# Forty-two sums of weight quarters on GpSimd instead of VectorE, under a new table of places for all instructions

## The chip, the cores and the metric

The kernel runs on one core of one Trainium2 chip. The metric is device time in microseconds (us) for one execution. TensorE (PE) multiplies, VectorE (DVE) and ScalarE (ACT) work element by element and move results out of PSUM, GpSimd (POOL) makes masks and issues some of the transfers, and SyncE (SP) issues the others. Each engine executes its instructions in the order in which the program lists them; what an instruction needs from another engine it waits for, and everything behind it on its engine waits with it.

## The reference

Threshold attention on 8 batches of 8 heads (576 positions, 64 columns a head), and behind it a feed-forward layer with a quick GELU on the 4608 rows that come out, all in float32:

```
scores = scale * np.matmul(q, k.transpose(0, 1, 3, 2))          # 8 x 8 x 576 x 576
thresh = np.max(scores, axis=-1, keepdims=True) - tau
scores = np.where(scores >= thresh, scores, -1000000000.0)
scores = scores - np.max(scores, axis=-1, keepdims=True)
attn = np.exp(scores)
attn = attn / (np.sum(attn, axis=-1, keepdims=True) + 1e-09)
x = np.matmul(attn, v)   -> rearranged to 4608 x 512
h = x @ w_in                                                    # 512 -> 2048
g = h * (1.0 / (1.0 + np.exp(-1.702 * h)))
return g @ w_out                                                # 2048 -> 512
```

## The kernel before, in words

**Attention.** The 64 heads are worked through as 32 pairs `n`, two heads at a time. For a pair, `scores` (L839) multiplies keys by queries into PSUM tiles `ps`; ACT copies them to SBUF (`keep`, L856), as five tiles `sT[n, t]`: four of 128x1152 and one of 128x576. DVE takes maxima of the tiles (`in_groups`, L879, into `part`), which become one row of thresholds for the pair; a transfer spreads that row over all partitions. Then each tile has the row added or subtracted: by DVE (`sub`, L961), or, for two of the five tiles in 25 of the pairs, by an accumulating DMA that GpSimd issues (`add_mb`, L954). Then ACT pushes everything below the threshold far down (`mask`, L968) and takes exponentials (`exps`, L972). PE multiplies them with the values into `pv`, and with ones into `den` (`by_values`, L983). DVE divides and writes the result into a tile `xT`, 128 x 4 x 256, one for each block of 256 rows; there are six such tiles. In the 25 pairs whose sums are not made by PE, DVE adds up the exponentials instead (L869).

**Feed-forward.** The 4608 rows are 18 blocks of 256. The layer `w_in` gives `hps`, ACT or DVE applies the GELU, and `w_out` gives `ops`. Blocks are multiplied with seven products in place of eight on half-size quarters (`P1` to `P7`), which needs sums and differences of quarters of the weights and of `x`. Lines L1163, L1174, L1238, L1411 and L1566 are products of the first layer, L1675 and L1719 of the second. While the pairs run (to about 950 us) blocks lie between the scores and values of the pairs and keep PE busy while the softmax of the next pair is on its way; from 950 us the last six blocks run alone (the tail, `TAIL` = 12). A PE that changes between 64x64 matmuls (scores, values) and 128x128 matmuls (feed-forward) does so in stretches: the order is scores and values mixed, then a stretch of feed-forward, then the next pair.

**The sums of weight quarters.** The tail uses a deeper form of the seven products, for which further sums of weight quarters are wanted: 7 for the first layer (`left1`) and 7 for the second (`right2`), each made by three additions or subtractions of 128x512. That is 14 x 3 = 42 operations, all in the function `scrap_sum` (L1464 to L1481). They are made between 280 and 810 us, and SP stores the results to DRAM (`extra_out`, `scrap_out`), from where the tail loads them (`extra_in`). Four of the fourteen are made beside blocks 2 and 3, in a free `xT` tile (`EARLY_EXTRAS`); ten beside blocks 4, 6, 8 and 10, in one tile `scrap` (`LATE_EXTRAS`), where each sum waits until the store of the one before has read the tile:

```
    nc.vector.tensor_tensor(out=o, in0=a, in1=b, op=op)          # L1481, the sum itself
    ...
    a = task("DVE", 0.6, FIRST, scrap_sum, second_layer, x, k, after=freed + [t_ready[-1], a])
    a = task("SP", 0.55, FIRST, scrap_out, second_layer, x, k, after=[a], take=RING[0])
```

**Weights at the start.** `w_in` and `w_out` come in through two staging tiles (`load_w`, L757, whose tiles the program calls `w_out` and `arena`), and are split into parts by `cv_...` steps on ACT and DVE, among them `cv_whole` (L785) and a step at L792 on DVE, L767 and L771 on ACT. All of this lies in the first 120 us.

**What sets the order.** All work is a list of tasks: engine, planned cost, rank, function, what it comes after, and which buffer it takes and gives back. `run_in_order` (L499) first writes a number from a table, `PLACES`, with 4767 entries, over the rank of each task, and then runs a planner: it simulates the engines with the planned costs, and each engine that is free takes the ready task with the lowest number. The instructions are issued in the order that comes out; the engines then run it as written, so the planned costs matter only through the order.

Of the kernel before, what the change touches and what calls it, by code (L numbers as in the profile page):

```python
# [21 lines left out]
P = 128  # L22
# [10 lines left out]
def kernel(  # L33
# [96 lines left out]
    for x in ("raw0", "raw1", "qkT0", "qkT1", "mb"):  # L130
# [113 lines left out]
        "keep1": 0.0,  # L244
        "keep4": 0.0,
# [7 lines left out]
        "silu4": 0.0,  # L253
        "x_sum": 0.0,
# [3 lines left out]
    STEP = {  # L258
        "add_mb": 0.0,
        "exps": 0.0,  # L260
        "in_groups": 0.0,
        "keep": 0.0,
        "mask": 0.0,
        "sub": 0.0,
# [14 lines left out]
    ENTER = {True: 0.2, False: 0.22}  # L279
# [27 lines left out]
    def transfer(by, time, a, kind=0, give=(), lag=1.7):  # L307
# [3 lines left out]

    PLACES = """
# [752 lines left out]
    def spread_sums(n):  # L1065
# [4 lines left out]
        nc.vector.transpose(out=rc, in_=r.unsqueeze(2).to_broadcast([P, QB, 32]))  # L1070
        rcs[n] = rc

    xTs = {}

    def cuts(b):

# [1776 lines left out]
```

## Time and profile before

| | |
|---|---|
| time, median of 3 runs | 1220.14 us (1217.45 to 1220.29) |
| profiled execution: time | 1220.53 us |
| profiled execution: span from the first to the last instruction | 1218.7 us, so 1.8 us lie outside |
| granted TensorE clock, mean | 0.997 of full speed |
| instructions in the span | 26167 |

The page is of one execution. A row of the list of groups reads: line of the code, engine, operation, written tile and read tiles with partitions x elements, number of instructions | busy us, mean ns of one | idle us of the engine just before them and what ended most of it. A row of the timeline reads: start in us, length in us, engine, line, operation, number of instructions in a row, and in square brackets how long the engine stood before it and what released it. A row of the stretches (windows) reads: from:to, length, then busy us (and number of instructions) of PE, PE's weight loads, DVE, ACT and POOL, then the granted clock, the busy share of the transfer engines and GB/s. A matmul in the trace is two records of a float32 matmul in the code. Names like `arena` and `w_out` are those of large tiles that hold many things in turn.

### The profile page before, as it was taken

How to read it: one execution, taken by the hardware profiler on the slowest of the kernel's cores; microseconds unless marked ns; L12 is line 12 of the kernel's file. 1: busy time of each engine (PE TensorE's matmuls, PEld its weight loads, DVE VectorE, ACT ScalarE, POOL GpSimd, SP SyncE). 2: the span in 40 equal slices, each digit the busy share in tenths (PEclk: the TensorE clock that was granted, in tenths of full speed). 3: DMA queues.
4: the chain of work that ended last, by engine and by line, in shares of the span. 5: the costliest groups of instructions: out<-in, count | busy, mean ns of one | idle time of the engine just before them, and what ended most of it. 6: DMA issues, size and time to landing. Idle time of an engine off the chain costs nothing.

```text
span 1218.7 us, 26167 instructions
## 1 busy us (share of the span) xinstructions
PE 1196.9 (98%) x10560; PEld 982.3 (81%) x10560; DVE 1067.9 (88%) x1622; ACT 794.1 (65%) x1183; POOL 130.5 (11%) x176
## 2 busy tenths in 40 slices
PE   9898999999999999999999999999999999999998
PEld 6555777788877778777777777777778999999998
DVE  7979998989989888999899877997896799799797
ACT  7999986888686868667875569667882340340340
POOL 0111232110001110012100110011100000000000
PEclk9999999999999999999999999999999999999999
DMA  9856869777555564567735653557623544545443
GB/s 246 227 114 167 205 144 178 150 149 206 132 131 120 132 150 103 126 146 178 152 71 127 168 123 66 142 119 203 159 60 122 181 124 149 172 131 148 141 138 96
DMA packets 220617, 176.56 MB, mean 145 GB/s; under 512 B 148752, under 2 KB 165776, under 8 KB 220368
## 3 DMA queue, kind: packets, MB, share of 16 engines
q1 hardware_dynamic: 197776, 125.42, 38.1%
q0 software_dynamic: 22032, 49.17, 20.2%
q8 instruction: 83, 1.36, 0.5%
q10 hardware_dynamic: 688, 0.30, 0.1%
q14 instruction: 38, 0.31, 0.1%
HBM read 119.53 MB, written 25.84 MB: 119 GB/s over the span
## 4 chain that ended last, share of the span: by engine, by line
PE 78%; ACT 14%; DVE 3%; DMA 3%; issue 2%; POOL 0%; SPq 0%; DVEq 0%; ACTq 0%; POOLq 0%
PE ops L1719 21%; PE pv L983 9%; PE ps L839 8%; PE hps L1411 8%; PE hps L1566 6%; PE ops L1675 6%; PE ps L1411 6%; PE ps L1566 5%; PE ps L1675 5%; ACT arena L968 4%; ACT arena L972 3%; ACT arena L856 2%; PE hps L1238 2%; PE ps L1238 1%; DVE arena L961 1%
## 5 line engine op out<-in xcount | busy, mean ns | idle before, releaser
L879 DVE TRANSPOSE_TENSOR_REDUCE part<-arena 128x36 f32<-128x1152 f32 (+1 forms) x250 | 297.3, 1212 | 21.4 <-ACT arena L856 15.0
L856 ACT COPY arena<-ps 128x576 f32<-128x576 f32 x288 | 171.5, 643 | 54.6 <-PE ps L839 52.1
L968 ACT ACTIVATE arena<-arena 128x1152 f32<-128x1152 f32 (+1 forms) x160 | 168.4, 1063 | 59.3 <-DVE arena L961 55.4
L972 ACT ACTIVATE arena<-arena,shift 128x1152 f32<-128x1152 f32 (+1 forms) x160 | 183.3, 1160 | 2.6
L839 PE MATMUL ps<-arena 64*64 64x288 f32 x2304 | 172.7, 409 | 7.8 <-ACT arena L856 6.2
L1719 PE MATMUL ops<-w_out,arena 128*128 128x256 f32 x768 | 174.6, 381 | 0.8 <-DVE osb L1741 0.4
L1719 PEld LDWEIGHTS ops<-w_out,arena 128*128 128x128 f32 x768 | 144.4, 190 | 26.9 <-issue 4.8
L983 PE MATMUL pv<-arena 64*64 64x288 f32 x2176 | 160.4, 407 | 0.0
L839 PEld LDWEIGHTS ps<-arena 64*64 64x64 f32 x2304 | 81.9, 133 | 70.9 <-ACT arena L856 29.1
L961 DVE TENSOR_TENSOR arena<-arena 128x1152 f32<-128x1152 f32 (+1 forms) x100 | 130.1, 1337 | 2.9 <-DMA arena<-row 2.2
L983 PEld LDWEIGHTS pv<-arena 64*64 64x64 f32 x2176 | 81.1, 133 | 52.7 <-issue 7.9
L1580 ACT COPY arena<-hps 128x512 f32<-128x512 f32 x66 | 38.5, 583 | 114.3 <-PE hps L1566 114.2
L1719 PE MATMUL ops<-arena 128*128 128x256 f32 x464 | 104.4, 380 | 0.7 <-ACT osb L1734 0.7
L954 POOL DMA_DIRECT2D arena<-arena x50 | 55.1, 1317 | 429.2 <-DVE arena L919 245.1
L1719 PEld LDWEIGHTS ops<-arena 128*128 128x128 f32 x464 | 87.9, 190 | 13.8 <-ACT osb L1734 1.1
L869 DVE TRANSPOSE_TENSOR_REDUCE part<-arena 128x72 f32<-128x2304 f32 x25 | 64.2, 2570 | 10.8 <-ACT arena L972 10.5
L1411 PE MATMUL hps<-xT,w_in 128*128 128x256 f32 x256 | 59.4, 382 | 0.1
L1741 DVE SCALAR_TENSOR_TENSOR osb<-ops,osb 128x256 f32<-128x256 f32 x84 | 33.5, 410 | 25.7 <-PE ops L1719 24.6
L1411 PEld LDWEIGHTS hps<-xT,w_in 128*128 128x128 f32 x256 | 48.1, 190 | 9.4 <-issue 2.6
L1452 ACT COPY arena<-hps 128x512 f32<-128x512 f32 x64 | 36.8, 578 | 26.7 <-PE hps L1411 26.5
L899 ACT ACTIVATE other<-red,gap 32x18 f32<-32x18 f32 x100 | 30.7, 307 | 35.9 <-DVE red L888 34.7
L1174 PE MATMUL hps<-xT,w_in 128*128 128x256 f32 x232 | 51.9, 382 | 1.9 <-DVE arena L1180 1.8
(223 smaller groups left out, 2056.8 us busy)
## 6 DMA issues: line engine op xcount, KB each, us to landing
arena<-in_v_dram SPq DMA_DIRECT2D x128, 144.0 KB
arena<-exu SPq DMA_DIRECT2D x63, 256.0 KB
arena<-ext SPq DMA_DIRECT2D x60, 256.0 KB
arena<-arena POOLq DMA_DIRECT2D x25, 576.0 KB, 6.1
arena<-wrow POOLq DMA_DIRECT2D x48, 256.0 KB, 4.5
arena<-in_q_dram SPq DMA_DIRECT2D x112, 72.0 KB
arena<-in_k_dram SPq DMA_DIRECT2D x112, 72.0 KB
arena<-arena POOLq DMA_DIRECT2D x25, 288.0 KB, 7.5
```

The source lines that it names most:

```text
L839: nc.tensor.matmul(ps[ts(c, KT), h, 0:SH], lhsT=mats[n, 1][ts(h, D), ts(j, KT)], rhs=mats[n, 0][ts(h, D), ts(c, SH)], start=True, stop=True,)
L856: nc.scalar.copy(out=sT[n, t][:, u], in_=pss.pop((n, j))[:, :, 0:SH])
L869: nc.vector.tensor_reduce(out=stats[n, ALU.add][:, t * 2 * QB : min(2 * t + 4, NK) * QB], in_=arena2[:, lo : mid + size].rearrange("p (c d ...
L879: nc.vector.tensor_reduce(out=stats[n, op][:, t * 2 * QB : min(2 * t + 2, NK) * QB], in_=sT[n, t].rearrange("p u h (g d) -> p (u h g) d", ...
L961: engine.tensor_tensor(out=s, in0=s, in1=mbs[n].unsqueeze(1).to_broadcast(list(s.shape)), op=ALU.add if n in BY_DMA or n in NEGATED else A ...
L968: nc.scalar.activation(out=s, in_=s, func=AF.Prelu, alpha=STEEP)
L972: nc.scalar.activation(out=s, in_=s, func=AF.Exp, scale=SCALE, bias=shift)
L983: nc.tensor.matmul(o[c][ts(h, D), 0:SH], lhsT=left(j, h)[ts(c, KT)], rhs=sT[n, t][ts(c, KT), u, h, :], start=(j == 0), stop=(j == NK - 1),)
L1411: nc.tensor.matmul(o[:, ts(j, BLK)], lhsT=left[:, c, ts(j, P)], rhs=right[:, c, :], start=(x in (P1, P2, P5) and j + c == 0), stop=(j + c ...
L1566: nc.tensor.matmul(o[:, ts(j, HT)], lhsT=left[:, ts(j, P)], rhs=right, start=(m in (P1, P2, P5) and j == 0), stop=(j == 3), skip_group_che ...
L1675: nc.tensor.matmul(banks3[pos, r][:, 0:HT], lhsT=left[:, j, :], rhs=right[:, j, :], start=(m in (P1, P2, P5) and j == 0), stop=(j == 3), s ...
L1719: nc.tensor.matmul(banks[blk][k][:, ts(o, HM)], lhsT=left[:, j, :], rhs=right[:, j, :], start=(j == 0), stop=(j == HF - 1),)
```

## The change

Three things change in the code.

1. The 42 operations of `scrap_sum` are issued on GpSimd, and their planned cost goes from 0.6 to 1.45.
2. The six `xT` tiles, until now handed out in turn by a pool, become six fixed tiles with a list of free ones (`x_free`): a user takes the first free one and its last user, by the planner, puts it back. Similarly the PSUM banks of one form of the first layer (`product4`, `keep4`) are remembered for each quarter `q` instead of two by turns.
3. The table `PLACES` is new throughout, so the order of nearly everything in the first half of the program is new; behind that the two orders are nearly alike apart from the sums; three of the planner's costs change with it (the transfer of the first two pieces of `w_out` is planned at 5.2 instead of 1.7, one transfer of a threshold row at 2.7 instead of 1.0, and entering one of the matmul modes at 0.0 instead of 0.2). Offsets for single tasks (`AT`) are emptied; `PLACES` overrides them in both programs.

Among the instructions themselves, only the 42 sums change: every engine but DVE and POOL issues the same instructions in another order. The summing of exponentials of two score tiles in one operation on DVE (`PAIRED`, 25 operations 128x72 from 128x2304) is the same in both programs.

```
 def scrap_sum(second, x, k):
 ...
-                places["extra", second, x] = x_home()
+                places["extra", second, x] = x_home((second, x))
 ...
-        nc.vector.tensor_tensor(out=o, in0=a, in1=b, op=op)
+        nc.gpsimd.tensor_tensor(out=o, in0=a, in1=b, op=op)
...
-                    "DVE", 0.6, FIRST, scrap_sum, second_layer, n, k,
+                    "POOL", 1.45, FIRST, scrap_sum, second_layer, n, k,
...
-                a = task("DVE", 0.6, FIRST, scrap_sum, second_layer, x, k, after=freed + [t_ready[-1], a])
+                a = task("POOL", 1.45, FIRST, scrap_sum, second_layer, x, k, after=freed + [t_ready[-1], a])
...
+    x_free, x_ends = list(range(NXT)), {}
...
+                x_free.extend(x_used.pop(key) for key in x_ends.get(i, ()) if key in x_used)
...
+    x_tiles = [const.tile([P, NDC, BLK], FP32, name=f"xT{x}") for x in range(NXT)]
+    x_used = {}
+
+    def x_tile(key):
+        x_used[key] = x_free.pop(0)
+        return x_tiles[x_used[key]]
...
-            places[y] = psM.tile([P, BANK], FP32, name="hps", tag="mo")
+            places["q", q] = psM.tile([P, BANK], FP32, name="hps", tag="mo")
...
-        a = transfer("DMS", W_TIME, a, 2, give=RING[0], lag=1.7 if i else 3.3)
+        a = transfer("DMS", W_TIME, a, 2, give=RING[0], lag=(5.2 if n_in <= i < n_in + 2 else 1.7) if i else 3.3)
...
-        rq = ("POOL", 1.4, "DMW", 1.0) if n in ROWS_BY_POOL else ("SP", 1.0, "DMS", 1.7)
+        rq = ("POOL", 1.4, "DMW", 2.7 if n == 1 else 1.0) if n in ROWS_BY_POOL else ("SP", 1.0, "DMS", 1.7)
...
-    ENTER = {True: 0.2, False: 0.22}
+    ENTER = {True: 0.0, False: 0.22}
...
     PLACES = """
-        114 170 133 238 4 92 157 188 151 49 8 600 155 191 299 353 83 365 180 203 376 143 354 391 326 212
+        20 104 357 14 328 8 81 136 28 23 123 411 41 138 74 150 19 381 57 140 184 223 174 384 99 152
```

What the new table moves is seen where the engines' instructions stand. Five places follow; each row is an operation with the tile it writes, the tiles it reads, the size and how many stand in a row. The line numbers of the changed program are 15 to 21 lower.

The first is SP's queue near 40 to 80 us, where the last pieces of `w_in`, the first two of `w_out` (L757, L736 in the changed program), and the keys, queries and values of the pairs are loaded. Before:

```order
L757 DMA w_out<-in_moe_w_in_dram 128x2047
L704 DMA arena_90<-in_q_dram 32x18x32 x4
L704 DMA arena_90<-in_k_dram 32x18x32 x4
L715 DMA arena_90<-in_v_dram 64x576 x4
L704 DMA arena_90<-in_k_dram 32x18x32 x4
L757 DMA w_out<-in_moe_w_out_dram 128x2047
L757 DMA arena<-in_moe_w_out_dram 128x2047
```

And after:

```order
L736 DMA w_out<-in_moe_w_in_dram 128x2047 x4
L694 DMA arena_90<-in_v_dram 64x576 x4
L736 DMA w_out<-in_moe_w_out_dram 128x2047
L736 DMA arena<-in_moe_w_out_dram 128x2047
L683 DMA arena_90<-in_k_dram 32x18x32 x2
L683 DMA arena_90<-in_q_dram 32x18x32 x4
L694 DMA arena_90<-in_v_dram 64x576 x4
```

The two loads of `w_out` now stand ahead of the next pair's keys and queries instead of behind them.

The second is DVE between 83 and 93 us, with the threshold subtractions of a pair (L961, L940 after) and the weight steps (L785 and L792, L771 after). Before:

```order
L792 SCALAR_TENSOR_TENSOR w_in<-w_out,w_in 128x512 x2
L792 SCALAR_TENSOR_TENSOR w_in<-arena,w_in 128x512
L961 TENSOR_TENSOR arena<-arena 128x1152
L785 TENSOR_SCALAR w_out<-w_out 128x512
L879 TENSOR_REDUCE part<-arena_90 128x36
L961 TENSOR_TENSOR arena<-arena 128x1152
L879 TENSOR_REDUCE part<-arena_90 128x18
L961 TENSOR_TENSOR arena<-arena 128x1152
```

And after:

```order
L771 SCALAR_TENSOR_TENSOR w_in<-arena,w_in 128x512
L940 TENSOR_TENSOR arena<-arena 128x1152
L771 SCALAR_TENSOR_TENSOR w_in<-arena,w_in 128x512
L940 TENSOR_TENSOR arena<-arena 128x1152 x2
L858 TENSOR_REDUCE part<-arena_90 128x36 x2
L858 TENSOR_REDUCE part<-arena_90 128x18
```

The first `cv_whole` of a `w_out` piece (L785 on tile `w_out`) no longer stands between the pair's subtractions.

The third is PE between 342 and 370 us: the end of a first-layer block (L1238, L1223 after), second-layer products `ops` (L1719, L1704 after), and the values `pv` (L983, L962 after) and scores `ps` (L839, L818 after) of the next two pairs. Before:

```order
L1238 MATMUL ps<-xT,arena_90 128x128 x16
L1719 MATMUL ops<-w_out,arena 128x256 x4
L983 MATMUL pv<-arena_90 64x288 x8
L839 MATMUL ps<-arena_90 64x288 x8
L983 MATMUL pv<-arena_90 64x288 x8
L839 MATMUL ps<-arena_90 64x288 x8
```

And after:

```order
L1223 MATMUL ps<-xT_95,arena_90 128x128 x16
L1704 MATMUL ops<-w_out,arena 128x256 x16
L962 MATMUL pv<-arena_90 64x288 x8
L818 MATMUL ps<-arena_90 64x288 x8
L962 MATMUL pv<-arena_90 64x288 x8
L818 MATMUL ps<-arena_90 64x288 x8
```

Sixteen matmuls of the second layer instead of four stand ahead of the pair's values; the twelve come from the stretch behind that pair, and eight 128x128 matmuls of this block have gone ahead of the pair before.

The fourth is POOL around 300 us, with the accumulating transfers of the thresholds (L954, L933 after). Before:

```order
L954 DMA arena_90<-arena_90 128x2x576
L954 DMA arena_90<-arena_90 128x576
L954 DMA arena_90<-arena_90 128x2x576
L954 DMA arena_90<-arena_90 128x576
```

And after:

```order
L1466 TENSOR_TENSOR xT_94<-arena_90 128x512
L1466 TENSOR_TENSOR xT_94<-xT_94,arena_90 128x512
L933 DMA arena_90<-arena_90 128x2x576
L933 DMA arena_90<-arena_90 128x576
L1466 TENSOR_TENSOR xT_94<-arena_90,xT_94 128x512
L1466 TENSOR_TENSOR xT_93<-arena_90 128x512
L933 DMA arena_90<-arena_90 128x2x576
L933 DMA arena_90<-arena_90 128x576
```

The sums stand between the transfers of the thresholds, which POOL issues in this order.

The last is the start of SP's queue, with the first piece of `w_in` (L757, L736 after) and the first pair's keys and queries. Before:

```order
L693 DMA arena_90<-in_k_dram 64x576
L693 DMA arena<-in_k_dram 64x576
L695 DMA arena_90<-in_q_dram 128x4x64
L699 DMA arena_90<-in_q_dram 64x64
L693 DMA arena<-in_k_dram 64x576
L757 DMA w_out<-in_moe_w_in_dram 128x2047
```

And after:

```order
L736 DMA w_out<-in_moe_w_in_dram 128x2047
L672 DMA arena_90<-in_k_dram 64x576
L674 DMA arena_90<-in_q_dram 128x4x64
L678 DMA arena_90<-in_q_dram 64x64
L672 DMA arena<-in_k_dram 64x576 x2
```

The load of the first weight piece now stands ahead of the first keys and queries.

More of the change, by code (lines that the diff above doesn't have):

```diff
@@ L243 @@
         "add4": 0.0,
-        "keep1": 0.0,
-        "keep4": 0.0,
         "read": 0.0,
@@ L253 @@
         "silu4": 0.0,
+        "keep1": 0.0,
+        "keep4": 0.0,
         "x_sum": 0.0,
@@ L258 @@
     STEP = {
+        "mask": 0.0,
+        "exps": 0.0,
+        "sub": 0.0,
+        "in_groups": 0.0,
         "add_mb": 0.0,
-        "exps": 0.0,
-        "in_groups": 0.0,
         "keep": 0.0,
-        "mask": 0.0,
-        "sub": 0.0,
     }
@@ L1084, in place_x @@
             if blk not in xTs:
-                xTs[blk] = work.tile([P, NDC, BLK], FP32, name="xT", tag="xT", bufs=NXT)
+                xTs[blk] = x_tile(("blk", blk))
             c = a // SH
@@ L1103, in x_in @@
     def x_in(blk):
-        xTs[blk] = work.tile([P, NDC, BLK], FP32, name="xT", tag="xT", bufs=NXT)
+        xTs[blk] = x_tile(("blk", blk))
         nc.sync.dma_start(out=x_flat(blk), in_=x_rows[blk])
@@ L1120, in mm1, with x_home @@
             )
-    def x_home():
-        t = work.tile([P, NDC, BLK], FP32, name="xT", tag="xT", bufs=NXT)
-        return t.rearrange("p c t -> p (c t)")
+    def x_home(key):
+        return x_tile(key).rearrange("p c t -> p (c t)")
     def tanh(j):
         if "th" not in places:
-            places["th"] = x_home()
+            places["th"] = x_home("th")
         ths[j] = places["th"][:, ts(j % 2, BANK)]
@@ L1404, in product4 @@
         if x == P1:
-            places[y] = psM.tile([P, BANK], FP32, name="hps", tag="mo")
+            places["q", q] = psM.tile([P, BANK], FP32, name="hps", tag="mo")
         elif x in (P2, P5) and y == 0:
             places["p2" if x == P2 else "p5"] = psA.tile([P, 2, 512], FP32, name="ps", tag="ps")
-        o = bank1(x, y)
+        o = bank1(x, y if x in (P2, P5, P3) else ("q", q))
         for j in range(2):
@@ L1451, in keep4 @@
         f, h = {P1: (0, 0), P6: (0, 1), P7: (1, 1), P4: (1, 0)}[x]
-        nc.scalar.copy(out=quarter4(q, f, h), in_=in_twos(bank1(x, q % 2)))
+        nc.scalar.copy(out=quarter4(q, f, h), in_=in_twos(bank1(x, ("q", q))))
     def add4(z, x):
@@ L1497, in loose_io @@
         if "io" not in loose:
-            loose["io"] = x_home()
+            loose["io"] = x_home("io")
         return loose["io"][:, ts(key == "x", BANK)]
@@ L1521, in extra_in @@
         if blk == TAIL and x == P2 and "b" not in loose:
-            loose["b"] = x_home()
+            loose["b"] = x_home("b")
             loose_io("a")
@@ L1871, in save_x @@
         saved[blk] = transfer("DMS", 2.8, a, 2, give=RING[0] + ("xT",))
+        x_ends[saved[blk]] = [("blk", blk)]
     def fetch_x(blk, xs):
@@ L1902, in first_blocks @@
                 ))
+                if j == NFC - 1:
+                    x_ends[ffn[-1]] = [("blk", i)]
             a = task("ACT", 0.48, FIRST, tanh, j, after=ffn[-1:], take=("io",) + (("xT",) if j == 0 else ()))
@@ L2220, in second2 @@
                     spread_on(y, dest[y])
-            m(P3, p5, [sums[3]], give=("xT", "xT") if x == P4 else ())
+            a = m(P3, p5, [sums[3]], give=("xT", "xT") if x == P4 else ())
+            if x == P4:
+                x_ends[a] = [("blk", blk), ("blk", blk + 1)]
             plus((0, 1), p5, give=("psA",))
@@ L2277, in seven @@
                     a = transfer("DMS", (3.0, 1.5)[k - 1], a, 2, give=RING[0] + (("xT",) if k == 2 else ()))
+                    if k == 2:
+                        x_ends[a] = [(second_layer, n)]
             (extra_out_done, extra2_out_done)[second_layer][n] = a
@@ L2295, in seven @@
                 ))
+                if x == P3 and y:
+                    x_ends[ffn[-1]] = [("blk", blk)]
                 if x == P1 and y:
@@ L2387, in seven4 @@
                     ))
+                    if x == P3 and q == 3:
+                        x_ends[ffn[-1]] = [("blk", blk), ("blk", blk + 1)]
                     if x in WC_OF:
@@ L2461, in alone @@
                 ))
+                if x == P3 and y:
+                    x_ends[ffn[-1]] = [("blk", blk)]
                 users.update((k, ffn[-1]) for k in turns)
@@ L2525, in second @@
             ))
+            if blk == 0 and x == P5 and p:
+                x_ends[ffn[-1]] = ["th"]
             if blk == 0 and x == P1 and p == 3:
```

390 rows, old and new, of tables (AT, PLACES) are left out of this document.

## The prediction, made before the changed kernel had run

> **What bounds the kernel now.** I read the page's busy times and its chain first, then the stretches of the trace, then the waits, and then the timeline around the two longest waits that the new order touches.
>
> ```profile
> PE 1196.9 (98%) x10560; PEld 982.3 (81%) x10560; DVE 1067.9 (88%) x1622; ACT 794.1 (65%) x1183; POOL 130.5 (11%) x176
> PE 78%; ACT 14%; DVE 3%; DMA 3%; issue 2%; POOL 0%; SPq 0%; DVEq 0%; ACTq 0%; POOLq 0%
> ```
>
> PE is busy for 98% of the span and carries 78% of the chain. DVE, which the change relieves, is 88% busy but holds 3% of the chain. The stretches say where PE is not full:
>
> ```profile
> 0.00:50.00 50.00, 45.37 (x708) 30.56 (x708) 39.42 (x56) 41.43 (x64) 7.68 (x23) 1.00 0.93 255
> 50.00:100.00 50.00, 43.32 (x564) 24.67 (x568) 41.66 (x69) 46.98 (x63) 5.91 (x8) 0.97 0.58 135
> 0.00:200.00 200.00, 185.15 (x2051) 127.33 (x2052) 176.63 (x265) 179.46 (x259) 41.60 (x68) 0.99 0.76 181
> 200.00:950.00 750.00, 746.50 (x6150) 590.34 (x6149) 653.12 (x838) 536.78 (x768) 88.88 (x108) 1.00 0.58 135
> 950.00:1219.00 269.00, 265.24 (x2363) 264.65 (x2361) 238.19 (x521) 77.86 (x157) 0.00 (x0) 1.00 0.48 145
> ```
>
> PE stands 14.85 us in the first 200, 3.5 in the next 750, and 3.8 in the tail. So in the part where the sums are made there are only 3.5 us of open standing to be won. A busy PE can still run slowly, because a matmul that is held at its operand counts as busy; that has to be read from pacing, below. Whom PE waits for:
>
> ```profile
> PE ps L839 <- ACT arena L856: 6.2, 12, 0.9
> PE den L983 <- ACT arena L972: 5.9, 5, 2.8
> POOL arena L954 <- DVE arena L919: 245.1, 10, 33.2
> ```
>
> The first two name ACT: its copies of scores and its exponentials. The third says that POOL stands most of the time waiting for DVE's thresholds.
>
> **The sums leave DVE.** The two rows are the 42 sums (L1481) and the threshold subtractions (L961) in the three stretches where the sums lie, 515 us in all:
>
> ```profile
> sum 515.00, DVE 27.42; mean DVE 9.14
> sum 515.00, DVE 70.91; mean DVE 23.64
> ```
>
> DVE loses 27.42 us, 0.653 a sum. With 97 us of 750 free on DVE already, and PE waiting for ACT rather than for DVE, I cost this at 0. It could give no more than the 3.5 us that PE stands in these 750.
>
> **The sums come to POOL.** The trace has no such sum on POOL. The nearest row of POOL with arithmetic is
>
> ```profile
> 1.42 0.29 POOL L1763 TENSOR_SCALAR_AFFINE_SELECT eye<-eye 128x128 f32<-128x128 f32 x1
> ```
>
> 0.29 us for 128 elements a partition and one input, so 1.16 for 512. Bounds: 0.65 (DVE's own) and 2.3 (twice the 1.16, for two inputs). I take 1.2, nearest to POOL's own row: 42 x 1.2 = 50 us, beside the 88.88 that POOL has in the 750. The sums are queued ahead of threshold transfers (L954), one to five in a row, so at worst 5 x 2.3 = 11.5 us late in front of a transfer; the transfers wait up to 33.2 us for L919, which gives POOL the time to have done its sums before. Cost 0. SP's stores of the sums wait for POOL instead of DVE; they have hundreds of microseconds until the tail.
>
> **Collisions on DVE.** Sums on POOL run beside subtractions on DVE, and both read two tiles of SBUF. If the one holds up the other: the subtractions fill 70.91 / 515 = 14% of the time, so of 42 sums some 42 x 0.14 = 6 start inside one, and as many subtractions start inside a sum (50 / 515 = 10% of 53). If each costs up to one sum, that is 6 x 1.2 = 7 us on DVE, of which, DVE having 13% free and standing off the chain, little reaches PE. I take 0.5, ends 0 and 7. The Trainium skill, "SBUF — State Buffer", section "Who interferes with whom", says more: a DVE instruction with two SBUF inputs contends with a GpSimd instruction that reads SBUF, and who issues first blocks the other for its whole length. The trace of before cannot show it; by that rule, the case is the third rival below rather than the 0.5. The page "GPSIMD Engine Reference", section 3.1, puts such an operation at about 2.6 cycles an element, an estimate of 1.1 us for 512, which would leave the sum here as it stands.
>
> **Place B, 360 us: more feed-forward ahead of a pair's values.**
>
> ```profile
> 346.11 3.74 PE L1238 MATMUL ps<-xT,arena 128*128 128x128 f32 x32
> 349.69 3.74 PE L1238 MATMUL hps<-xT,w_in 128*128 128x128 f32 x32
> 359.55 1.28 ACT L972 ACT_TABLE_LOAD   x1
> 359.68 1.15 PE L839 MATMUL ps<-arena 64*64 64x288 f32 x16
> 360.64 1.15 PE L983 MATMUL pv<-arena 64*64 64x288 f32 x16
> 362.68 0.72 PE L839 MATMUL ps<-arena 64*64 64x288 f32 x8 [0.88 <-ACT arena L856]
> 364.27 1.07 PE L839 MATMUL ps<-arena 64*64 64x288 f32 x8 [0.88 <-ACT arena L856]
> 365.10 2.16 PE L983 MATMUL pv<-arena 64*64 64x288 f32 x16
> 367.02 1.35 PE L839 MATMUL ps<-arena 64*64 64x288 f32 x12
> 403.29 3.45 PE hps L1411 x16
> ```
>
> The clean pace is 359.68 to 360.64: 0.96 us for 16. From 360.64 to 367.02 PE takes 6.38 us for 48, which at that pace are 2.9: 3.5 lost, of which 1.76 show as waits. ACT is the cause: it loads the exponentials' table only at 359.55, behind the block's GELU, and copies scores between exponentials. In the new order 12 more products of the second layer stand ahead of these values (24 records of 3.45 / 16 = 0.216: 5.18 us) and 8 fewer 128x128 (16 records at (349.69 - 346.11) / 32 = 0.112: 1.79). PE comes 3.4 us later to the values, and ACT has 3.4 more ahead. That covers nearly all the loss: -3.4 us (between 0, if the next pair pays, and -3.5).
>
> **Place A, 91 us: loads of w_out earlier.**
>
> ```profile
> 79.95 0.35 SPq L757 DMA_DIRECT2D w_out<-in_moe_w_out_dram  x1
> 84.80 1.35 DVE L961 TENSOR_TENSOR arena<-arena 128x1152 f32<-128x1152 f32 x1
> 89.78 0.43 DVE L785 TENSOR_SCALAR w_out<-w_out 128x512 int32<-128x512 uint32 x1 [3.62 <-DMA w_out<-in_moe_w_out_dram]
> 91.33 1.15 PE L983 MATMUL pv<-arena,arena 64*64 64x288 f32 x16
> 91.42 1.31 DVE L961 TENSOR_TENSOR arena<-arena 128x1152 f32<-128x1152 f32 x1
> 92.77 1.16 ACT L968 ACTIVATE arena<-arena 128x1152 f32<-128x1152 f32 x1 [2.62 <-DVE arena L961]
> 95.27 2.20 PE L983 MATMUL den<-arena,ones 64*64 64x288 f32 x16 [2.79 <-ACT arena L972]
> 98.72 1.14 PE L983 MATMUL den<-arena,ones 64*64 64x288 f32 x16
> ```
>
> DVE stands 3.62 us for a piece of `w_out` that SP issued at 79.95; queued behind it is a pair's subtraction (91.42), behind that the mask and exponentials on ACT, and then PE, which waits 2.79 and takes 98.72 - 91.33 = 7.39 us for 48 records worth 2.9: 4.5 lost. After the change SP issues this load ahead of a pair's keys and queries instead of behind them, and that step of DVE no longer stands between the subtractions. What comes late next is ACT: it is 46.98 of 50 us busy in this stretch, so it can give back only the 2.62 that it stood here. I take -2.6 (ends 0 and -4.5). The transfers that the loads overtake serve a later pair; bounds of that are within the same ends.
>
> **The start.**
>
> ```profile
> 0.74 1.22 SPq L693 DMA_DIRECT2D arena<-in_k_dram  x2
> 4.20 0.35 SPq L757 DMA_DIRECT2D w_out<-in_moe_w_in_dram  x1
> 4.55 1.95 PE L817 MATMUL ps<-eye,arena 64*64 64x64 f32 x36
> w_out<-in_moe_w_in_dram SPq DMA_DIRECT2D x12, 511.8 KB
> ```
>
> PE's first work waits for the first keys. The first load of `w_in` now goes ahead of them: at least its issue, 0.35, and at most that plus 511.8 KB at the stretch's 255 GB/s, 2.0, together 2.4. I take +0.8, nearer to the issue, since transfers of two loads run beside each other.
>
> **Mode changes.** By the two orders PE changes between 64x64 and 128x128 matmuls 80 times instead of 76, the four more in the first 200 us.
>
> ```profile
> 340.03 0.69 PE L839 MATMUL ps<-arena 64*64 64x288 f32 x8
> 342.54 3.74 PE L1238 MATMUL hps<-xT,w_in 128*128 128x128 f32 x32
> ```
>
> Between these starts lie 2.51 us; the work is 8 records of the one (0.48) and 16 of the other (1.79), so a change costs 0.24. Four are 1.0; in a stretch where PE stands anyhow I take +0.3 (0 to 1.0).
>
> Tile handing (`x_free`), banks by quarter, planner's costs: they act through the order alone, 0. The tail has the same rows in nearly the same order, 0.
>
> **Sum.** -3.4 (B) - 2.6 (A) + 0.8 + 0.3 + 0.5 = -4.4, against the profiled execution's own 1220.53: 1216.1. That execution is 0.4 above the median of 1220.14 and inside the runs shown. I say 1216; the ends of all terms added give 1220.5 - 8.0 - 3.5 = 1209 and 1220.5 + 2.4 + 1.0 + 7 = 1231.
>
> **Rivals.** *Nothing gained (0.22).* The stall at B moves on: the next pair has 40 instead of 48 products of the second layer ahead of its values, 16 records x 0.216 = 3.45 us less cover, just what the first pair gained. And at A a full ACT gives nothing. For it speaks that ACT is what both waits name; against it that the stall is not known to exist at the next pair. Then 1220.5 + 0.8 + 0.3 + 0.5, less about 2.6 from A or nothing: 1219.5 to 1222.
>
> *Slower by collisions (0.28).* At 2.3 us a sum, 97 us of sums lie beside the subtractions, 97 / 515 = 19% of 53: 10 subtractions stand for up to a sum each, and 6 sums for a subtraction, which delays the threshold transfer queued behind on POOL. 10 x 2.3 / 2 = 12 us on DVE in front of ACT's masks. It decides if a sum takes 2.3 or more and half of that reaches PE: 1220 + 6 = 1226. The skill's rule on the shared port speaks for this; the 97 us free on DVE and the waits that name ACT speak against.
>
> *More gained (0.12).* All of A and B and half of PE's other standing in the first 200 us goes: -4.5 - 3.5 - 3.5 = 1209.
>
> The forecast itself has 0.38. Faster by over 0.3% (3.7 us, below 1216.5; about what a measurement of this kernel tells from no change) is 0.38 + 0.12 = 0.50, within it 0.22, slower (above 1223.8) 0.28. The range 1209 to 1226 leaves out the far half of the collisions and little below; the forecast's own is 1213 to 1217.
>
> **What would show it.** The 42 sums are rows of POOL of about 1.2 us and are gone from DVE, whose busy time falls by some 27. Around 360 us the values follow at 0.96 for 16 without ACT waits; if they stand at the next pair instead, the first rival holds. At 80 to 100 us no wait of L785's successor for the load stands ahead of the subtractions. PE's first matmul starts at about 5.3. If subtractions on DVE in 280 to 810 us grow beyond 1.34 on average, collisions are real. The prediction is wrong if the new order opens a wait in the first 200 us that neither place shows, since nearly every row there is moved, or if sums take well over 2 us.

## The result and the profile after

The changed kernel takes 1230.61 us (median of 6 runs, 1229.1 to 1232.33), the kernel before 1219.56 us (6 runs). The ratio is 1.0090, with an interval of 1.0076 to 1.0104: slower by 0.9%, where 1216 us had been forecast. The profiled execution took 1230.61 us, with a span of 1228.8 us.

From the page of the changed kernel: the busy times, and the groups of the threshold subtractions and of the accumulating transfers (L961 and L954 of before are L940 and L933 here).

```profile
PE 1198.3 (98%) x10560; PEld 981.5 (80%) x10560; DVE 1071.8 (87%) x1580; ACT 796.5 (65%) x1183; POOL 188.2 (15%) x218
...
L940 DVE TENSOR_TENSOR arena<-arena 128x1152 f32<-128x1152 f32 (+1 forms) x100 | 147.2, 1507 | 0.9
...
L933 POOL DMA_DIRECT2D arena<-arena x50 | 55.4, 1319 | 300.3 <-issue 135.9
```

VectorE has 42 instructions fewer (1580 for 1622) and is busy no less: 1071.8 us for 1067.9. About as much as the 27.42 us that left it came back elsewhere. The largest piece: the same 100 subtractions take 147.2 us, where they took 130.1 (the L961 row of the list of groups before). The rest, some 10 us, lies in other operations of VectorE with two inputs in SBUF, such as additions of 128x1024 that take 1.22 us alone and up to 2.86 beside a sum. The stretches of the changed kernel, with the same columns as before, say where PE stands:

```profile
0.00:200.00 200.00, 184.35 (x2055) 126.36 (x2056) 177.90 (x266) 180.19 (x260) 41.64 (x68) 1.00 0.77 182
200.00:950.00 750.00, 738.27 (x6097) 581.25 (x6096) 653.62 (x785) 537.93 (x767) 146.58 (x150) 1.00 0.57 135
```

In the 750 us in which the sums are made PE stands 11.7 us instead of 3.5; in the first 200 us it is as before. The list of single subtractions (duration in ns: shortest, median, longest; then first and last start in us) shows what is new:

```profile
L940 DVE TENSOR_TENSOR arena<-arena x100: 751/1352/5132, 22.6 to 921.7; 128x1152 f32<-128x1152 f32 x98, 128x576 f32<-128x576 f32 x2
```

The median is unchanged at 1.352 us (1.350 before), but the longest took 5.13 us. This is where that one lies, on the timeline of the changed kernel:

```profile
316.11 0.78 DVE L898 STREAM_TRANSPOSE arena<-red 128x576 f32<-128x576 f32 x1
316.93 8.75 DVE L940 TENSOR_TENSOR arena<-arena 128x1152 f32<-128x1152 f32 x3
317.43 2.15 POOL L933 DMA_DIRECT2D arena<-arena  x2 [17.29 <-issue]
318.76 3.62 PE L1704 MATMUL ops<-w_out,arena 128*128 128x256 f32 x16
318.78 2.10 POOL L1466 TENSOR_TENSOR xT<-xT,arena 128x512 f32<-128x512 f32 x1
320.02 2.09 POOL L1466 TENSOR_TENSOR xT<-arena 128x512 f32<-128x512 f32 x1
322.19 2.28 POOL L1466 TENSOR_TENSOR xT<-xT,arena 128x512 f32<-128x512 f32 x1
325.61 0.74 DVE L1726 SCALAR_TENSOR_TENSOR osb<-ops,osb 128x256 f32<-128x256 f32 x2
326.40 3.80 PE L1223 MATMUL hps<-xT,w_in 128*128 128x128 f32 x18 [4.02 <-DVE osb L1726]
```

Three subtractions, 8.75 us instead of some 4. Behind them on VectorE stands L1726, which empties a PSUM bank, and PE waits 4.02 us for that bank. The order of events is no accident. VectorE's L898 spreads the thresholds of the pair; the subtractions, next on VectorE, read what it wrote, and so do the transfers of L933, at which POOL stands 17.29 us. (The row names no releaser for that wait; that the transfers read this tile is in the code.) The sum that stands behind the transfers on POOL therefore starts when the subtractions have just begun. In the whole trace ten sums meet and stretch a subtraction: seven stand directly behind threshold transfers, one has a transfer of weights in between, and two follow the first sum above without a pause. Three more sums stand directly behind threshold transfers and stretch no subtraction; nor does any of the other 29.

The waits of PE, as a list of the changed kernel:

```profile
PE hps L1223 <- DVE osb L1726: 4.0, 1, 4.0
PE hps L1396 <- ACT arena L1437: 3.1, 1, 3.1
PE ops L1704 <- DVE osb L1726: 2.8, 2, 1.5
```

The first lies at 326 us, the second at 417, and 1.51 of the third at 390, each behind subtractions that were stretched. (The other 1.25 of the third lies at 208 us, ahead of the first sum.)

To compare places, I give for each trace the time PE has lost when it has done a given amount of work: the start of the matmul that reaches that amount, less the amount itself at the clean pace (0.060 us for a record of 64x288, 0.112 for 128x128, 0.216 for 128x256). It is worked out from all matmul records of the traces; the 352 records of other forms count little, and only differences between columns or rows are read from it. "Before again" is a second profile of the unchanged kernel (run e7 below), "gated" is run e6.

| work done, us | before | before again | changed | gated |
|---|---|---|---|---|
| 50 | 30.1 | 29.9 | 31.8 | 31.5 |
| 75 | 39.5 | 37.8 | 38.7 | 38.4 |
| 275 | 47.3 | 46.2 | 46.8 | 46.2 |
| 300 | 47.8 | 46.6 | 53.1 | 46.6 |
| 325 | 52.1 | 49.5 | 53.8 | 47.3 |
| 375 | 53.0 | 50.5 | 61.7 | 50.1 |
| 1152 (all) | 63.6 | 61.1 | 74.1 | 60.2 |

Up to 275 us of work the changed kernel is as fast as before. Between 275 and 375 it loses 14.9 us, where before lost 5.7 in its first profile and 4.3 in the second.

### The profile page after: what moved, and what is told of

Read it like the earlier page. It is cut to its first block, busy times and chain, and to the rows that moved or that the text cites. A ratio compares the mean times of both kernels' runs of the same rounds, so it can differ in the third digit from the quotient of the medians.

```text
span 1228.8 us, 26224 instructions
## 1 busy us (share of the span) xinstructions
PE 1198.3 (98%) x10560; PEld 981.5 (80%) x10560; DVE 1071.8 (87%) x1580; ACT 796.5 (65%) x1183; POOL 188.2 (15%) x218
## 3 DMA queue, kind: packets, MB, share of 16 engines
q8 instruction: 83, 1.36, 0.5%
## 4 chain that ended last, share of the span: by engine, by line
PE 52%; DVE 2%; ACT 1%; issue 1%; DMA 0%; DVEq 0%; ACTq 0%
PE ops L1704 10%; PE hps L1396 7%; PE ops L1660 6%; PE hps L1551 6%; PE ps L1396 5%; PE pv L962 5%; PE ps L1551 5%; PE ps L1660 5%; PE ps L818 4%; DVE arena L940 1%; ACT arena L951 0%; DVE part L858 0%; ACT arena L947 0%; DVE osb L1726 0%; DMA arena<-in_v_dram 0%
## 5 line engine op out<-in xcount | busy, mean ns | idle before, releaser
L818 PE MATMUL ps<-arena 64*64 64x288 f32 x2304 | 172.2, 408 | 7.2 <-ACT arena L835 5.0
L1704 PE MATMUL ops<-w_out,arena 128*128 128x256 f32 x768 | 173.7, 381 | 1.2 <-DVE osb L1726 1.2
L1704 PEld LDWEIGHTS ops<-w_out,arena 128*128 128x128 f32 x768 | 144.7, 190 | 25.8 <-issue 2.6
L962 PE MATMUL pv<-arena 64*64 64x288 f32 x2176 | 158.8, 405 | 1.0 <-DVE arena L806 1.0
L940 DVE TENSOR_TENSOR arena<-arena 128x1152 f32<-128x1152 f32 (+1 forms) x100 | 147.2, 1507 | 0.9
L818 PEld LDWEIGHTS ps<-arena 64*64 64x64 f32 x2304 | 81.1, 132 | 71.0 <-ACT arena L835 30.3
L962 PEld LDWEIGHTS pv<-arena 64*64 64x64 f32 x2176 | 80.2, 133 | 54.2 <-issue 6.6
L1704 PE MATMUL ops<-arena 128*128 128x256 f32 x464 | 105.2, 381 | 2.7 <-DVE osb L1726 1.5
L1704 PEld LDWEIGHTS ops<-arena 128*128 128x128 f32 x464 | 87.5, 190 | 17.5 <-DVE osb L1726 2.6
L933 POOL DMA_DIRECT2D arena<-arena x50 | 55.4, 1319 | 300.3 <-issue 135.9
L848 DVE TRANSPOSE_TENSOR_REDUCE part<-arena 128x72 f32<-128x2304 f32 x25 | 64.3, 2574 | 16.8 <-ACT arena L951 16.8
L1373 POOL DMA_DIRECT2D arena<-wrow x48 | 31.0, 661 | 156.7 <-PE hps L1396 58.3
```

The lines of the kernel that those rows point to most:

```text
L818: nc.tensor.matmul(ps[ts(c, KT), h, 0:SH], lhsT=mats[n, 1][ts(h, D), ts(j, KT)], rhs=mats[n, 0][ts(h, D), ts(c, SH)], start=True, stop=True,)
L848: nc.vector.tensor_reduce(out=stats[n, ALU.add][:, t * 2 * QB : min(2 * t + 4, NK) * QB], in_=arena2[:, lo : mid + size].rearrange("p (c d ...
L940: engine.tensor_tensor(out=s, in0=s, in1=mbs[n].unsqueeze(1).to_broadcast(list(s.shape)), op=ALU.add if n in BY_DMA or n in NEGATED else A ...
L962: nc.tensor.matmul(o[c][ts(h, D), 0:SH], lhsT=left(j, h)[ts(c, KT)], rhs=sT[n, t][ts(c, KT), u, h, :], start=(j == 0), stop=(j == NK - 1),)
L1704: nc.tensor.matmul(banks[blk][k][:, ts(o, HM)], lhsT=left[:, j, :], rhs=right[:, j, :], start=(j == 0), stop=(j == HF - 1),)
```

## The experiments

The ratio of each row is to the kernel before run beside it on the same chip. The rows were measured on several chips, on which the median of the kernel before lay between 1218.6 and 1219.6 us, so two rows are best compared by their ratios:

| run | what | median us | ratio, 95% interval |
|---|---|---|---|
| changed | all 42 sums on GpSimd, new order | 1230.61 | 1.0090 (1.0076 to 1.0104) |
| e1 | new order, sums on VectorE | 1223.97 | 1.0033 (1.0021 to 1.0046) |
| e2 | old order, sums on GpSimd | 1228.33 | 1.0070 (1.0053 to 1.0086) |
| e3 | new order, fills instead of sums | 1217.17 | 0.9985 (0.9972 to 0.9998) |
| e4 | new order, 10 sums on VectorE, 32 on GpSimd | 1218.28 | 0.9989 (0.9978 to 0.9999) |
| e5 | new order, copies instead of sums | 1217.46 | 0.9992 (0.9979 to 1.0005) |
| e6 | new order, all sums on GpSimd, 8 gated | 1218.11 | 0.9999 (0.9990 to 1.0008) |
| e7 | before, one more profile | 1217.96 (one run) | |
| e8 | e6 with the first keys ahead of the first weights | 1218.50 | 1.0006 (0.9997 to 1.0015) |
| e9 | old order, 14 sums on VectorE, 28 on GpSimd | 1219.55 | 1.0009 (1.0000 to 1.0018) |

**e1: the new order with the sums on VectorE.**

```
-        nc.gpsimd.tensor_tensor(out=o, in0=a, in1=b, op=op)     # changed kernel, scrap_sum
+        nc.vector.tensor_tensor(out=o, in0=a, in1=b, op=op)
```

> The changed kernel's order on every engine, with the 42 sums issued on VectorE again at the points where the new order has them (PE's order is unchanged). Theory (collisions: sums on GpSimd hold up VectorE's two-input subtractions): subtractions back at 1.35 us each (135 us for the 100 instead of 147.2), the PE waits at 320, 385-390, 413 and 471 us gone; they cost about 14 us in the trace, so 1216 to 1218 us. Rival (the new order itself is slower, whichever engine makes the sums): 1228 to 1231 us.

Measured: 1223.97 us, between the two theories. The subtractions are back:

```profile
L940 DVE TENSOR_TENSOR arena<-arena x100: 730/1352/1374, 24.2 to 916.4; 128x1152 f32<-128x1152 f32 x98, 128x576 f32<-128x576 f32 x2
```

So some 7 us of the difference go with the engine of the sums alone (1.0090 against 1.0033). But both theories missed: with the sums on VectorE the new order is some 4 us slower than the old one. The new order as such does not explain that, since e3, e4 and e6, with PE's same order, take 1217 to 1218 us. In this profile, the slowest of the six runs (1225.38 us), some 3 us were lost at 204 us, ahead of the first sum, to a threshold row that came late: VectorE's L1073, which waits for it there, waited 4.00 us in e1, 2.62 in e6 and 1.36 in e4.

```profile
206.76 0.95 DVE L1073 TENSOR_TENSOR xT<-pv,arena 128x192 f32<-128x192 f32 x4 [4.00 <-DMA arena<-row_s]
...
203.87 0.95 DVE L1073 TENSOR_TENSOR xT<-pv,arena 128x192 f32<-128x192 f32 x4 [1.36 <-DMA arena<-row_s]
```

(The first row is of e1, the second of e4.) Some 4 us more are lost in pieces below 2 us from 280 to 560 us of work, where VectorE now does the sums at points that the order had chosen with the sums on another engine. That this is what the pieces come from is likely, but no run separates it, and whether the late row belongs to this order or to this one execution was not tried either.

**e2: the old order with the sums on GpSimd.** The same line of `scrap_sum` in the kernel before, the other way round.

> The kernel before, only the 42 sums issued on GpSimd at the points where the old order had them on VectorE. Theory (collisions): subtractions above 1.35 us in places where a sum lies beside them, 5 to 12 us slower, 1225 to 1232 us; if the sums in the old order happen to miss the subtractions, nearer to the lower end. Rival (the new order is what is slower): 1219 to 1221 us.

Measured: 1228.33 us, 9 us slower than before although nothing else is changed and PE's order is the same. The new order is not needed for the loss. The same picture as above, in the old order:

```profile
314.30 5.16 DVE L961 TENSOR_TENSOR arena<-arena 128x1152 f32<-128x1152 f32 x2
314.80 2.15 POOL L954 DMA_DIRECT2D arena<-arena  x2 [13.81 <-issue]
...
316.15 2.09 POOL L1481 TENSOR_TENSOR xT<-arena 128x512 f32<-128x512 f32 x1
```

**e3: work on GpSimd that reads nothing.**

```
-        nc.gpsimd.tensor_tensor(out=o, in0=a, in1=b, op=op)
+        nc.gpsimd.memset(o, 0.0)
+        nc.gpsimd.memset(o, 0.0)
```

> The changed kernel, but each of the 42 sums is replaced by two fills of the same 128x512 tile with zeros on GpSimd, which read nothing from SBUF (the sums of weight quarters are left out). Theory (it is GpSimd's reading beside a two-input instruction of VectorE that locks): no subtraction above 1.36 us though the fills lie beside them, 1216 to 1218 us. Rival (any GpSimd work in these places does it, by holding up what is queued behind it on GpSimd, or by writing): 1226 to 1231 us.

Measured: 1217.17 us, and no subtraction is longer than 1.361 us, although 20 of them had a fill beside them:

```profile
L940 DVE TENSOR_TENSOR arena<-arena x100: 747/1352/1361, 23.2 to 907.2; 128x1152 f32<-128x1152 f32 x98, 128x576 f32<-128x576 f32 x2
```

The fills occupied the same places in POOL's queue (84 of them, 52.2 us, against 65.8 us of sums). So it is neither the queue nor writing that costs, and the rival falls. It was rather the fills that were longer: the first fill behind the transfers, begun inside a subtraction, took 1.36 to 1.42 us in eight places, where most others take 0.52. Whether the subtraction or the transfers ahead of it did that is not separated.

**e4: only the sums that met a subtraction go back.**

```
+        back = {
+            (0, P5): (1,), (0, P3): (0, 1), (0, P4): (0, 2), (1, P1): (0,), (1, P2): (2,),
+            (0, P7): (0,), (1, P7): (1,), (1, P3): (1,),
+        }
+        engine = nc.vector if k in back.get((second, x), ()) else nc.gpsimd
-        nc.gpsimd.tensor_tensor(out=o, in0=a, in1=b, op=op)
+        engine.tensor_tensor(out=o, in0=a, in1=b, op=op)
```

> The changed kernel, but the 10 sums that lay beside a threshold subtraction in its trace are issued on VectorE, the other 32 stay on GpSimd. Theory (the loss comes from those few sums): 1217 to 1221 us, with total busy time of the 100 subtractions at most 140 us. Rival (every sum on GpSimd costs its share): 10 of 42 back give a quarter of the loss, 1226 to 1228 us.

Measured: 1218.28 us. Ten of 42 sums carry some 12 us of the time; 32 on GpSimd cost nothing that can be measured. The longest subtraction is 1.365 us.

```profile
L940 DVE TENSOR_TENSOR arena<-arena x100: 746/1352/1365, 23.1 to 907.9; 128x1152 f32<-128x1152 f32 x98, 128x576 f32<-128x576 f32 x2
```

**e5: one read instead of two.** `nc.gpsimd.tensor_copy(out=o, in_=a)` in place of the sum.

> The changed kernel, but each of the 42 sums is one copy of its first operand on GpSimd (it reads one tile of SBUF instead of two; the sums of weight quarters are left out). If GpSimd's reading is what locks: subtractions that a copy meets are again longer than 1.36 us, by about the length of a copy, and the time lies between the 1217.2 of fills and the 1230.6 of sums, about 1222 to 1228. Rival (only an operation with two inputs on GpSimd locks): no subtraction above 1.36 us, 1216 to 1219 us.

Measured: 1217.46 us, with the longest subtraction at 2.151 us.

```profile
L940 DVE TENSOR_TENSOR arena<-arena x100: 751/1351/2151, 24.3 to 908.6; 128x1152 f32<-128x1152 f32 x98, 128x576 f32<-128x576 f32 x2
```

One read is enough to stretch a subtraction: eight that a copy met took 1.76 to 1.77 us, 0.41 longer. But a copy (some 0.61 us alone) costs far less than a sum, and the time I had expected was wrong. My reading, which no run separates, is that pieces of 0.4 us disappear in the waits that are there anyhow, and a stretch by a sum, of 2 us and more, does not.

**e6: all 42 sums on GpSimd, but not beside the subtractions.**

```
+    BEHIND = {
+        (0, P5, 1): 11, (0, P4, 0): 13, (0, P4, 2): 14, (1, P1, 0): 16,
+        (1, P2, 2): 17, (0, P7, 0): 21, (1, P7, 1): 22, (1, P3, 1): 26,
+    }
...
+        if (second, x, k) in BEHIND:
+            nc.gpsimd.tensor_copy(out=after_sub, in_=sT[BEHIND[second, x, k], 2][:, 1, 1, 0:1])
         nc.gpsimd.tensor_tensor(out=o, in0=a, in1=b, op=op)
```

The copy of one column makes POOL wait for the pair's last subtraction. The order of PE, VectorE, ScalarE and SyncE is that of the changed kernel; on GpSimd one transfer of weights is issued ahead of a gated sum instead of behind it.

> The changed kernel with all 42 sums on GpSimd and every other engine's order unchanged; ahead of eight sums GpSimd copies one column of the pair's third score tile, which makes it wait until VectorE has finished that pair's subtractions. Theory (the cost is the meeting of sums and subtractions, caused by the threshold transfer that the sum stands behind): the subtractions are back at 1.35 us, 1217 to 1219 us. Rival (sums on GpSimd cost time wherever they are, or the gate holds up transfers behind it): 1224 us or more.

Measured: 1218.11 us, 12.5 us less than the changed kernel by the medians and 11 by the ratios. The place of the first timeline, now:

```profile
316.25 3.90 DVE L944 TENSOR_TENSOR arena<-arena 128x1152 f32<-128x1152 f32 x3
316.75 2.15 POOL L937 DMA_DIRECT2D arena<-arena  x2 [17.18 <-issue]
320.21 0.18 POOL L1477 COPY after_sub<-arena 128x1 f32<-128x1 f32 x1 [1.31 <-DVE arena L944]
320.35 1.28 POOL L1478 TENSOR_TENSOR xT<-xT,arena 128x512 f32<-128x512 f32 x1
321.54 3.73 PE L1227 MATMUL hps<-xT,w_in 128*128 128x128 f32 x32
```

The three subtractions take 3.90 us instead of 8.75, the sum waits 1.31 us behind the gate, and PE goes on without a stop. This is the experiment that settles it: same instructions (and eight small copies), same engines, all but the same order, only the meeting with the subtractions is taken away. The other two-input operations of VectorE are still stretched, by some 9 us in all against some 10 in the changed kernel, and that costs nothing that shows: what counts is what stands behind the operation that is held up.

**e7: the kernel before, profiled once more.**

> The kernel before, unchanged, for a second profile. If the stalls at 91 us and 360 us are fixed parts of the old order, both are there again with 4.5 and 3.5 us lost. Rival (they were partly the luck of one execution): at least one is smaller by a microsecond or more.

Measured: one run at 1217.96 us. Both stalls are there again, and both are smaller:

```profile
88.36 0.43 DVE L785 TENSOR_SCALAR w_out<-w_out 128x512 int32<-128x512 uint32 x1 [2.40 <-DMA w_out<-in_moe_w_out_dram]
...
93.85 1.20 PE L983 MATMUL den<-arena,ones 64*64 64x288 f32 x16 [1.57 <-ACT arena L972]
...
359.49 1.15 PE L983 MATMUL pv<-arena 64*64 64x288 f32 x16
361.52 0.71 PE L839 MATMUL ps<-arena 64*64 64x288 f32 x8 [0.89 <-ACT arena L856]
363.12 0.72 PE L839 MATMUL ps<-arena 64*64 64x288 f32 x8 [0.88 <-ACT arena L856]
363.65 1.15 PE L983 MATMUL pv<-arena 64*64 64x288 f32 x16
```

At 91 us VectorE stood 2.40 us for the load instead of 3.62, and PE waited 1.57 us instead of 2.79. At 360 us the two waits are the same, but the matmuls behind them run at the clean pace again: 4.16 us for 32 records worth 1.9, so 2.2 lost instead of 3.5. So the rival holds: the profile on which the prediction rested was of an execution that lost more at both places than the next one did.

**e8: keys first at the start.** In the gated kernel, the first load of `w_in` is issued behind the first pair's first set of keys and queries.

> The gated kernel of the run before last, with the first load of w_in issued behind the first pair's first keys and queries instead of ahead of them. If the start costs what the traces show (PE's first product of the pair at 6.70 instead of 4.55 us) and nothing later gives it back: 1.5 to 2.1 us below the gated kernel. Rival (what PE wins at the start it loses on the weight steps before 75 us): within 0.7 us of it.

Measured: 1218.50 us, 0.4 above the gated kernel: the rival's time holds, but not its reason. PE's first product of the pair, in the changed kernel and then in e8:

```profile
6.70 1.51 PE L796 MATMUL ps<-eye,arena 64*64 64x64 f32 x32 [2.09 <-DMA arena<-in_k_dram]
```

```profile
4.28 1.26 PE L805 MATMUL ps<-eye,arena 64*64 64x64 f32 x36
5.47 0.66 PE L802 MATMUL ps<-eye,arena 128*128 128x128 f32 x4
6.06 0.33 PE L805 MATMUL ps<-eye,arena 64*64 64x64 f32 x4
9.29 0.32 PE L805 MATMUL ps<-eye,arena 64*64 64x64 f32 x2 [2.90 <-DMA arena<-in_k_dram]
```

PE starts 2.4 us earlier, and then waits 2.90 us for the next keys, so the gain is gone by 9.3 us. What PE lost by 25 us of work is 26.4 us here and 25.5 in the gated kernel.

**e9: the old order with the relief alone.** As e4, in the kernel before, with the 14 sums that had stretched a subtraction in e2 on VectorE.

> The kernel before with its own order; of the 42 sums the 14 that met a threshold subtraction when all were on GpSimd stay on VectorE, the other 28 go to GpSimd. It takes some 18 us of work off VectorE without the meetings. Theory (PE does not wait for VectorE's load as such, so the relief is worth nothing): 1217.5 to 1220 us, ratio within 0.2% of before, subtractions at 1.35 us. Rival (the relief is worth something and only the meetings hid it): 1216 us or less. Third (sums on GpSimd cost something even where they meet no subtraction): 1222 us or more.

Measured: 1219.55 us, ratio 1.0009 (1.0000 to 1.0018). VectorE is 645.27 us busy in the 750, where the unchanged kernel has 651.86 (e7), so the relief is of 6.6 us, and PE does not gain. (No subtraction was above 1.359 us; some 7 of the 18 us came back all the same, since the remaining sums stretched other two-input operations, such as an addition of 1.21 us to 3.07.) The two rows are e9 and e7:

```profile
200.00:950.00 750.00, 746.15 (x6149) 588.97 (x6148) 645.27 (x809) 536.33 (x767) 124.78 (x136) 1.00 0.58 135
...
200.00:950.00 750.00, 746.22 (x6156) 590.43 (x6155) 651.86 (x838) 535.24 (x766) 87.88 (x107) 1.00 0.59 136
```

Taking sums off VectorE is worth nothing in the old order, because PE does not wait there for VectorE's load. In the new order it is not so: e4 differs from e1 only in that 32 sums have left VectorE, and is 5.7 us faster, of which the late row in e1's profile may be up to 3. Of all these, e3 apart, which leaves the sums out, only e4 lies below the kernel before by its interval, and by some 0.1%; no version clearly beats it.

## Why the prediction was wrong

**The step that failed is "Collisions on DVE", which was put at 0.5 us and is 11 to 12.5** (changed less gated kernel, by the ratios and by the medians). The mechanism was named, as a term and as the rival on the slow side (the second in its list, though the text calls it the third), which came to 1226 us; its size was wrong in two factors.
- *How often.* I counted meetings as if sums and subtractions lay independently: 14% of 42, 6 sums. Ten met, by cause and not by chance: eight stand on POOL behind transfers that wait for the very thresholds that start the subtractions, and two behind the first of these. The prediction looked at this queue, and only asked whether the sums make the transfers late. It did not ask what releases the sum that stands behind.
- *How much.* I allowed one sum, 1.2 us, for a meeting. A subtraction in which a sum began took 3.6 to 4.0 us in four places, 2.2 to 2.6 more than its 1.35, and 5.13 with three sums behind each other; in three more places the next subtraction took 1.58 to 2.43. That is not idle time of VectorE that slack can take up: L1726, which frees PE's bank, and the exponentials stand right behind.

The Trainium skill, "SBUF — State Buffer", section "Who interferes with whom", speaks of just this pair of instructions, and that only a GpSimd instruction that reads SBUF contends. e3 (fills: no subtraction above 1.361 us), e5 (copies: 1.76) and the sums (up to 5.13) agree with it. What the traces do not bear out is the other half that the prediction took from there, that who issues first blocks the other: the subtraction at 413.39 us had begun 0.61 us ahead of the sum and took 3.98 all the same. By the rule on reads the rival on the slow side deserved most of the chance, not 0.28.

**The price of a sum on POOL** was right: 1.27 us undisturbed, against 1.2 taken; the ten that met a subtraction took 2.07 to 2.28. The rival on the slow side was tied to a sum of 2.3 us or more; it did not need that.

**The sums leaving VectorE at 0**: right in the old order, as far as e9 tests it. In the new order it is not 0: with all sums on VectorE (e1) that order is 0.33%, some 4 us, slower than the old one, and with the sums on GpSimd and out of the way (e6) it is as fast. The prediction added this term and the order's terms as if each were worth the same without the other, and they are not.

**The order's terms, -4.9 together** (B, A, the start, the mode changes): measured with the sums off VectorE, the gated kernel against before, 0.9999 (0.9990 to 1.0008), so 0 within 1.2 us; with the sums on VectorE, e1, they come to +4.0 (2.6 to 5.6). In the table of lost time, against the second profile of before:
- *Place B, -3.4.* Right in kind: the stall is gone, and 32 records of the second layer now stand ahead of the values (the rows are of the changed kernel):

```profile
362.15 7.07 PE L1704 MATMUL ops<-w_out,arena 128*128 128x256 f32 x32
369.15 1.20 PE L962 MATMUL pv<-arena 64*64 64x288 f32 x16
370.17 1.15 PE L818 MATMUL ps<-arena 64*64 64x288 f32 x16
```

  It was worth 3.6 us against the first profile and 2.2 against the second. And between 325 and 375 us of work the gated kernel loses 2.8 us where before lost 0.9. There PE waits for ScalarE's copy of a feed-forward product (L1441) behind masks and exponentials; it is the first rival's thought, a stall that moves on, at another instruction than it named. The row is of the gated kernel:

```profile
410.38 1.99 PE L1400 MATMUL hps<-xT,w_in 128*128 128x256 f32 x8 [1.41 <-ACT arena L1441]
```

- *Place A, -2.6.* The stall is gone there too: from 50 to 75 us of work the gated kernel loses 6.9 us, before 9.4 in the first profile and 7.9 in the second. So the term is 2.5 or 1.0, by the execution one compares with.
- *The start, +0.8, and the modes, +0.3.* At 50 us of work the gated kernel is 1.4 to 1.6 us behind before, against the 1.1 forecast. The first load ahead of the keys is not the cause, as e8 shows: with it moved back, nothing is won. What else of the new order costs this was not tried.

So the order did what was forecast at its two places and, with the sums off VectorE, still sums to nothing. The places were chosen where the one profile had its largest stalls, which is where a second execution is likely to be better.

## What to carry to other kernels

Before moving element-wise work to GpSimd, list the two-input instructions of VectorE that it can run beside, and look at what releases it: work queued on GpSimd behind a wait starts when that wait ends, so it meets whatever the same event starts on VectorE. In this kernel the cost was set by a few meetings and by what stood behind them, not by the total of either engine, and one small dependency that lets VectorE finish first took it away. A stall that is to be won back should be read from two executions, not one.

## What the runs showed of the hardware that I had not expected

- A sum of 128x512 on GpSimd, 1.27 us undisturbed, that begins inside a subtraction of 1.35 us can stretch it to 3.6 to 4.0 us: more than the two after each other (2.6). The sum itself then takes 2.08 to 2.14 us. In other places (at 507.9 and 778.5 us of the changed kernel) the subtraction in which the sum began kept its 1.35 us, and the next was stretched, to 2.43 and 1.58 us. What decides between the two was not found.
- A copy of the same size on GpSimd, with one read, stretched a subtraction by 0.41 us in eight places and by 0.80 in one, and fills did not stretch it at all.
- The one-input reductions of VectorE were not touched. The longest kind, 128x72 from 128x2304 (L848), took 2.574 us on average in the changed kernel, with sums beside eight of the 25, and 2.570 before:

```profile
L848 DVE TRANSPOSE_TENSOR_REDUCE part<-arena 128x72 f32<-128x2304 f32 x25 | 64.3, 2574 | 16.8 <-ACT arena L951 16.8
```

- For the same transfer of a row at 204 us VectorE stood between 1.36 and 4.00 us in three executions, of programs that are alike up to there; the latest cost PE some 3 us in that execution.
